# Attention with a relative bias and an ELU MLP: the second chunk pair made from seven products, and four smaller edits

## The chip, the cores and the metric

One Trainium2 chip, one of its cores. The metric is the time of one execution on the device in microseconds. The kernel before took 662.24 us (median of 3 runs, 661.66 to 663.11).

## The reference, cut to what matters

```python
# q, k, v: (4 batches, 8 heads, 576 positions, 64)
scores = matmul(q, k.T) / 8
x = log1p(|i - j|) / log1p(max(i, 1))                  # positions i, j
bias = relu(x * w1 + b1) @ w2                          # 32 hidden, one value per head
attn = softmax(scores + bias)
x = matmul(attn, v)                                    # -> 2304 tokens x 512
h = x @ w_in                                           # 512 -> 2048
g = where(h > 0, h, exp(min(h, 0)) - 1)
out = g @ w_out                                        # 2048 -> 512, float32
```

## The kernel before, in words

The work has three stages, one after another on the same engines. The order of instructions on each engine is the order in which the program writes them; the framework adds the waits and gives out buffers.

**Bias (`bias_phase`).** 36 sets of 16 rows each. For a set, four relu operations (L220 on ScalarE, L222 on VectorE, DVE for short; `LEAN` lists the sets of which ScalarE makes two instead of one), matmuls that mix the 32 hidden values into 8 heads (`mix`, L230), a scaled copy out of PSUM (`place`, L243, ScalarE) and a transfer into the bias tile (L251 for a set alone, L263 for two together). The last set goes head by head.

**Attention (`attention`).** 16 head pairs, one step each. A step is five strings of tokens (`FIRST` for the first pair, `STEPS` and `LATE` for the others, `LAST` behind the last pair); each token is a method. `S` makes scores on PE, `X` adds the bias and takes the extreme on DVE (L359) and the exponential on ScalarE (L370), `T` transposes on PE into two of three PSUM banks (the pool "w"), `P` copies those out on ScalarE (A) or DVE (V), `M` and `Q` do so for the middle columns, `V` multiplies by v, `C` copies the result. `a` means the pair of this step, `y` the one before. After each string `aside` adds more: for every fourth pair the sums of a batch are inverted and transposed (`lift`, `invert`, `turn`; L390 on PE, L392 on DVE) and stored. The tokens low, scale, sign, shift and add decode one float64 weight chunk per step (L313 and L326 on GpSimd, L317 to L323 on DVE); the result is stored to DRAM (L328, SP). Loads of decoded weights are `load_w` (L558); a weight is split into a high part on ScalarE (`high_w`, L561) and a low part on DVE (`low_w`, L565), because matmuls run in a reduced-precision format with three products per pair of operands.

**MLP (`mlp`).** Three token blocks of 768 (two halves of 384), each with 8 chunk pairs i, 24 pairs in all. The first `FIRST` pairs take `eight`: four blocks of x @ w_in, 12 matmuls each, from weights that attention has split. All others take `seven`: seven products of sums, 6 matmuls each, of sums of weight blocks (A11, A12, A22, S1 to S4, made by `make_w`: L824 to L829 the sums on DVE into the tile S, L821 the high parts on ScalarE, L822 the low parts on DVE) and sums of x (T1 to T4; L542, L551, L554). `make_w` is cut by `yield`, and `at(i, k, ...)` puts each piece behind product k of pair i. After a product come the ELU's steps: L899 and L900 on ScalarE, L893 (maximum) on DVE, the high copy to g L894 on ScalarE, the low part L888 on DVE, one or two products later. The matmuls with w_out (`second`, L865) of pair i - 1 fill in between the products of pair i; pair 0 has none to fill in. `seven` uses two PSUM tiles, "h0" and "h1", one buffer each: its first, third and the maximum of its third product free the tile of its fifth. Made weights are stored to DRAM (L846, L847) and fetched again in the second and third block (L803). The weight rings, "S" and "wa" of the pool wq lie where tiles of attention lay.

Of the kernel before, what the change touches and what calls it, by code (L numbers as in the profile page):

```python
# [11 lines left out]
F32R = mybir.dt.float32r  # L12
# [12 lines left out]
def kernel(  # L25
# [11 lines left out]
    nc = tc.nc  # L37
    B, HP, D, _, S = qT.shape
    NT, DM = out.shape
    H = 2 * HP  # L40
    P = 128
    NCH = S // P
# [8 lines left out]
    WW = 2 * DM  # L51
# [6 lines left out]
    keep = ctx.enter_context(tc.tile_pool(name="keep", bufs=2))  # L58
# [86 lines left out]
    def bias_phase():  # L145
        with (
# [8 lines left out]
            NS = S // 16  # L155
# [49 lines left out]
            sets = [(2 * o + y, s) for s in range(4) for y in range(2) for o in range(2)]  # L205
            sets += [(2 * o + y, s) for o in (2, 3) for s in range(4) for y in range(2)]
            sets[16:16] = [(2 * NCH, s) for s in range(4)]
            LEAN = 1, NS - 6, NS - 5, NS - 4
            rels, pss = {}, {}

            def relu(s):
                B, x = sets[s]
                rels[s] = []
                for g in range(4):
# [3 lines left out]
                    rel = (bw0, bw1, bw2)[s % 3].tile([P, S], F32, tag="rel", name="rel")  # L218
                    if g < (2 if s in LEAN else 1):
                        nc.scalar.activation(rel, src, AF.Relu, bias=b)  # L220
# [17 lines left out]
            def place(s):  # L238
                if s % 2 == 0:
                    pss["bo"] = bop.tile([P, 2, S], F32, tag="bo", name="bo")  # L240
                bo = pss["bo"]
                B, x = sets[s]
                nc.scalar.activation(  # L243
                    bo[:, s % 2].rearrange("p (f x) -> p f x", f=2), pss.pop(s)[:, :, 0:HS],
                    AF.Copy, scale=inv[:, B, x:x + 1],
                )
                if NCH <= B < 2 * NCH:
                    q0 = 64 * (B % 2) + x
                    dst = bias[q0:q0 + 61:4, B // 4, :, B // 2 % 2]
                    if s < NS - 1:  # L250
                        nc.sync.dma_start(out=dst, in_=bo[:, s % 2])  # L251
                        return
                    src = bo[:, s % 2].rearrange("(k h) x -> k h x", h=H)
                    parts = [(dst[:, h], src[:, h]) for h in range(H)]
                    later.extend(parts[2:])
                    send(parts[:2])
                    return
                if s % 2 == 0:
                    return
                B, x = sets[s - 1]  # L260
                if B < NCH:
                    q0 = 64 * (B % 2) + x
                    nc.sync.dma_start(out=bias[q0:q0 + 61:4, 0], in_=bo)  # L263
                    return
                for e in range(2):
                    src = bo.rearrange("(i e) s x -> i e s x", e=2)[:, e]
                    for o in range(2):
                        q0 = TAIL * e + x + o
                        nc.sync.dma_start(out=biast[q0:q0 + 61:4], in_=src[:, o])
# [109 lines left out]
    def invert(b):  # L379
        sm = st["sm", b].rearrange("p h u -> p (h u)")  # L380
        nc.vector.reciprocal(sm, sm)
# [174 lines left out]
    def load_w(fc, pool=None):  # L556
        wa = wab[fc] = (pool or keep).tile([P, WW], F32, tag="wa", name="wa", bufs=2)
        nc.sync.dma_start(out=wa, in_=wf[fc])  # L558

    def high_w(fc):  # L560
        nc.scalar.copy(ws[fc][0], wab[fc])  # L561

    def low_w(fc, eng):
        hi, lo = ws[fc]
        eng.tensor_sub(lo, wab.pop(fc), hi.bitcast(F32))  # L565


    room = bias.rearrange("p c h t x -> p (c h t x)").bitcast(F32R)
    RW = NCH * H * S
# [3 lines left out]
    for fc in range(4):  # L573
        o = RW // 2 + 2 * fc * WW
# [3 lines left out]
    def attention():  # L578
# [14 lines left out]
        )  # L593
        FIRST = (
            "aS0 aS4 aX00 aX01 high rest aX40",
            "aS1 aX10 aX11",
            "aS2 aT0 w3 aP00A aX20 aX21 aP01V",
            "aS3 aT1 w3 aX30 aX31 aP10V",
            "zS0 aT4 aP11V aP40A aP41A",
        )  # L600
        SECOND = (
# [9 lines left out]
        )  # L611
        LAST = (
            "yM0 yQ0V yT2 yP20A yP21V yV00 yV01 low",
            "yT3 yP30A yP31V yV02 yV03 sign yM1 yQ1A yV04 yC0V shift",
            "yV10 yV11 yV12 yV13 yV14 yC1A",
        )
        late = []

        V, G = nc.vector, nc.gpsimd
# [98 lines left out]
        def aside(n, i):  # L718
            if i == 1:
                weights(n - 2, "store")  # L720
            if i == 0 and n > 0:
                load_v(n)
                pad_v(n - 1)
            if i == 2:
                if 0 < n < NP - 2:
                    load_pair(n + 2)
            if n == 0 and i == 1:
                open_banks()
            if n > 0 and n % HP == 0:
                if i == 0:  # L730
                    lift(n // HP - 1)
                if i == 1:
                    invert(n // HP - 1)
                if i == 2:
                    late.extend(turn(n // HP - 1))
            others(n, i)
            if n < NP - 1:
                return
            if i == 0:
                load_w(0)  # L740
                load_w(1)
            if i == 2:
                high_w(0)
            if i == 3:
                low_w(0, nc.vector)
            if i == 4:
                load_w(2)
                high_w(1)
# [9 lines left out]
        pad_v(NP - 1)  # L758
        step(NP, LAST[0])
        invert(B - 1)  # L760
        step(NP, LAST[1])
        late += turn(B - 1)
        step(NP, LAST[2])
        others(NP, 1)
        low_w(1, nc.vector)
        flush()
        load_w(3)
        weights(NP - 1, "store")
        high_w(2)
        low_w(2, nc.vector)  # L770

    def mlp():
        ep = ctx.enter_context(tc.tile_pool(name="ep", bufs=3))
# [3 lines left out]
        wq = ctx.enter_context(tc.tile_pool(name="wq", bufs=1))  # L777
# [4 lines left out]
        AN, GN = 2 * 7 * AW, 4 * DM  # L782

        wrings = [
            [wq.tile([P, AN], F32R, name="wA0")] + [room[:, o:o + AN] for o in (RW // 2, RW // 2 + 4 * WW)],
            [wq.tile([P, GN], F32R, name=f"wB{i}") for i in range(3)],
        ]
        wA = [dpool.tile([P, AN], F32, name=f"wA{q}") for q in range(NQ)]
        wB = [dpool.tile([P, GN], F32, name=f"wB{q}") for q in range(NQ)]
        NP2 = NB * NQ  # L790
        FIRST = 2


        def place_w(i, kind):
# [54 lines left out]
        acc, count, g = {}, {}, {}  # L849


        def second(i, order):
            j = i // NQ
            for e, h in order:
                gh, gl = g[i, e]
                wh, wl = (
                    [ws[2 * i + e][f][:, DM:] for f in range(2)] if i < FIRST else [W2[i][:, f, e] for f in range(2)]
                )
                for t in range(3 * h, 3 * h + 3):
                    if (j, t) not in acc:  # L860
                        acc[j, t] = accp.tile([P, DM], F32, tag="acc", name="acc")
                        count[j, t] = 0
                    for x, w in ((gh, wh), (gh, wl), (gl, wh)):
                        count[j, t] += 1
                        nc.tensor.matmul(  # L865
                            acc[j, t],
                            lhsT=x[:, t * P:(t + 1) * P],
                            rhs=w,
                            start=(count[j, t] == 1),
                            stop=(count[j, t] == 6 * NQ),  # L870
                        )
                        if count[j, t] == 6 * NQ:
                            os = ep.tile([P, DM], F32, tag="os", name="os", bufs=4)
                            (nc.scalar.copy if t % 2 else nc.vector.tensor_copy)(os, acc[j, t])
                            t0 = 2 * j * HB + t * P
                            (nc.scalar if t % 2 else nc.sync).dma_start(out=out[t0:t0 + P, :], in_=os)
                        yield


# [98 lines left out]
        def at(i, k, fn, *args):  # L978
            plans.setdefault((i, k), []).append((fn, args))

        V, G = nc.vector, nc.gpsimd
# [2 lines left out]
        free = [slots[8], slots[1]]  # L984
        at(0, 0, sums_x, 0, ("T2",), V)
        at(0, 1, sums_x, 0, ("T4",), V)
        at(0, 1, high_w, 3)
        at(0, 2, low_w, 3, V)
        for (m, k), name in (((0, 2), "T2"), ((0, 3), "T3"), ((1, 1), "T1"), ((1, 2), "T4")):
            at(m, k, high_x, 0, name, xo[name], nc.scalar.copy)  # L990
            at(m + (k + 1) // 4, (k + 1) % 4, low_x, 0, name, xo[name], V)

        for i in range(FIRST, NQ + FIRST):
            q = i % NQ
            run = make_w(i)
            for e in range(2):
                at(i - 2, 0 if i - 2 < FIRST else 2, load_w, 2 * q + e, wq if i % 2 == 0 else keep)
            for k in (0, 0, 1, 2, 3, 3, 3) if i == FIRST else (0, 1, 2, 3, 4, 5, 6):
                at(i - 1, k, next, run)
            at(i, 0, next, run)  # L1000
            at(i, 1, next, run)
            at(i, 3, next, run, None)
# [14 lines left out]
        for j in range(1, NB):  # L1017
            o = (j - 1) * NQ
# [16 lines left out]
        for i in range(NP2):  # L1035
            j, q = divmod(i, NQ)
# [84 lines left out]
```

## Time and profile before

| what | value |
|---|---|
| median of 3 runs | 662.24 us |
| the profiled execution | 660.94 us, span 659.2 us |
| PE busy | 643.9 us (98%) |
| DVE busy | 479.5 us (73%) |
| ScalarE (ACT) busy | 449.6 us (68%) |
| GpSimd (POOL) busy | 142.7 us (22%) |
| granted TensorE clock | 0.999 |

The rows further down come from one profiled execution; times are microseconds from the start of its span. A row of a timeline gives start, duration, engine, line, operation, tiles and shapes, and in brackets how long the engine stood idle before and what ended that. A row of the chain gives start, length and the work that the end of the kernel was waiting for at that time. SPq and ACTq are the queues that issue transfers.

### The profile page before, as it was taken

Reading aid. Unit: us, or ns where it says so; the run is one execution under the profiler, and the core shown is the slowest. Engines: PE = TensorE matmul, PEld = TensorE weight load, DVE = VectorE, ACT = ScalarE, POOL = GpSimd, SP = SyncE. Lnnn points to the kernel's source line nnn. Section 1 sums busy time; section 2 is a strip of 40 time slices with the busy share of each in tenths; the row PEclk is TensorE's granted clock in tenths of the full one; section 3 lists DMA queues with packets and bytes.
Section 4 is the critical chain, followed back from the end, with each engine's and each line's share of the span. In section 5 each row is a group of like instructions: output and inputs, shape, how many; then the busy total and the mean of one; then the engine's idle time right before and its main releaser. Section 6 shows DMA issues by size and latency. Waiting matters only on the chain.

```text
span 659.2 us, 14000 instructions
## 1 busy us (share of the span) xinstructions
PE 643.9 (98%) x5316; PEld 517.3 (78%) x5316; DVE 479.5 (73%) x993; ACT 449.6 (68%) x981; POOL 142.7 (22%) x207
## 2 busy tenths in 40 slices
PE   6988999999999999999999999999999999999997
PEld 3335777777777677799998889899899899899896
DVE  7998888898888988986778998554466554444443
ACT  6999999999999899685666676544345544444443
POOL 1002666656665667500000000000000000000000
PEclk9999999999999999999999999999999999999999
DMA  6999677776888676546798678977854565444102
GB/s 166 215 223 253 178 206 235 245 235 206 227 269 235 190 200 219 204 174 213 252 360 291 240 254 337 373 265 239 279 211 191 198 254 231 184 178 176 65 0 96
DMA packets 47139, 144.42 MB, mean 219 GB/s; under 512 B 9936, under 2 KB 22624, under 8 KB 39392
## 3 DMA queue, kind: packets, MB, share of 16 engines
q1 hardware_dynamic: 45584, 140.88, 65.6%
q10 hardware_dynamic: 1488, 2.65, 1.1%
q8 instruction: 42, 0.69, 0.4%
q14 instruction: 25, 0.20, 0.1%
HBM read 91.92 MB, written 40.97 MB: 202 GB/s over the span
## 4 chain that ended last, share of the span: by engine, by line
PE 89%; ACT 6%; DMA 2%; issue 1%; SPq 1%; DVE 0%; ACTq 0%
PE acc L865 30%; PE h L914 27%; PE wv L468 13%; PE ps L339 11%; PE wt L427 6%; ACT rel L220 3%; ACT bo L243 3%; PE wm L401 1%; PE acc L914 1%; PE wt L435 1%; DMA bias<-bo 1%; DMA T<-in_rtab_dram 0%; DMA kk<-in_k_dram 0%; DMA out_dram<-os 0%; PE spin L707 0%
## 5 line engine op out<-in xcount | busy, mean ns | idle before, releaser
L865 PE MATMUL acc<-wB,gh 128*128 128x512 f32 x528 | 171.3, 392 | 0.0
L914 PE MATMUL h<-bias 128*128 128x384 f32 x552 | 111.4, 338 | 0.0
L865 PEld LDWEIGHTS acc<-wB,gh 128*128 128x128 f32 x528 | 98.1, 188 | 14.3
L359 DVE CUSTOM_DVE_ANT_0 ss<-ps,bias 128x576 f32<-128x576 f32 x128 | 91.8, 754 | 22.3 <-PE ps L339 10.9
L914 PEld LDWEIGHTS h<-bias 128*128 128x128 f32 x552 | 99.8, 188 | 7.5 <-issue 0.4
L865 PE MATMUL acc<-wB,gl 128*128 128x512 f32 x264 | 103.8, 393 | 0.0
L370 ACT ACTIVATE ss<-ss,nm 128x576 f32<-128x576 f32 x128 | 99.3, 778 | 5.1 <-DVE nm L359 4.8
L894 ACT CAST gh<-e 128x384 fp32r<-128x384 f32 x96 | 49.4, 514 | 39.8 <-DVE e L893 38.8
L899 ACT ACTIVATE e<-c 128x384 f32<-128x384 f32 x66 | 34.7, 525 | 53.4 <-DVE c L945 53.4
L888 DVE TENSOR_TENSOR gl<-e,gh 128x384 fp32r<-128x384 f32 x96 | 53.2, 554 | 19.0 <-ACT gh L894 16.6
L899 ACT ACTIVATE e<-h 128x384 f32<-128x384 f32 x28 | 13.8, 491 | 69.4 <-PE h L914 68.5
L893 DVE SCALAR_TENSOR_TENSOR e<-e,c 128x384 f32<-128x384 f32 x66 | 36.8, 557 | 30.6 <-ACT e L900 30.5
L914 PE MATMUL h<-bias,wA 128*128 128x384 f32 x276 | 56.3, 338 | 0.0
L865 PEld LDWEIGHTS acc<-wB,gl 128*128 128x128 f32 x264 | 49.5, 187 | 7.8
L914 PEld LDWEIGHTS h<-bias,wA 128*128 128x128 f32 x276 | 50.2, 188 | 3.8
L900 ACT ACTIVATE e<-e 128x384 f32<-128x384 f32 x96 | 50.5, 526 | 3.0
L945 DVE TENSOR_TENSOR c<-h,u 128x384 f32<-128x384 f32 x66 | 36.7, 556 | 20.1 <-PE h L914 20.1
L230 PE MATMUL bps<-rel,cs 128*32 128x288 f32 x576 | 43.9, 424 | 6.4 <-ACT rel L220 1.7
L427 PEld LDWEIGHTS wt<-ident,ss 64*128 64x128 f32 x1024 | 41.0, 138 | 10.9 <-issue 7.0
L427 PE MATMUL wt<-ident,ss 64*128 64x64 f32 x1024 | 46.7, 227 | 1.1 <-DVE nm L359 0.4
L373 POOL TENSOR_SCALAR md<-ss 128x128 f32<-128x128 f32 x64 | 21.9, 342 | 116.6 <-ACT ss L370 112.7
L339 PE MATMUL ps<-kh,qh 64*128 64x288 f32 x256 | 45.5, 341 | 0.1
(139 smaller groups left out, 1203.0 us busy)
## 6 DMA issues: line engine op xcount, KB each, us to landing
wB<-wB SPq DMA_DIRECT2D x22, 1024.0 KB, 5.2
raw<-in_wd_dram SPq DMA_DIRECT2D x16, 1024.0 KB, 6.4
bias<-wA SPq DMA_DIRECT2D x9, 1792.0 KB, 9.2
wA<-wA SPq DMA_DIRECT2D x8, 1792.0 KB, 8.7
wa<-wf SPq DMA_DIRECT2D x20, 512.0 KB, 4.4
wA<-bias SPq DMA_DIRECT2D x5, 1792.0 KB, 9.0
wf<-da SPq DMA_DIRECT2D x16, 512.0 KB, 7.0
qq<-in_q_dram SPq DMA_DIRECT2D x32, 144.0 KB, 6.2
```

The source lines that it names most:

```text
L230: nc.tensor.matmul(ps[32 * g:32 * g + 32, f, 0:HS], lhsT=W2, rhs=rel[g][:, f * HS:(f + 1) * HS], start=True, stop=True,)
L339: nc.tensor.matmul(ps[:, f, 0:HS], lhsT=(qh, ql)[q][r, u * P:(u + 1) * P] if u < NCH else qd[n % 2][q], rhs=k[r, f * HS:(f + 1) * HS], sta ...
L359: nc.vector.tensor_tensor_reduce(out=s.rearrange("p (f x) -> p f x", f=2), in0=st["ps", n, u][e][:, :, 0:HS], in1=bap.rearrange("p (f x) - ...
L370: nc.scalar.activation(s, s, AF.Exp, bias=nm, scale=-1.0, accum_out=st["sm", b][:, hp, col:col + 1])
L427: nc.tensor.transpose(banks[r][:, x * TAIL:(x + 1) * TAIL], ss[q, c:c + P], ident[q, q])
L468: nc.tensor.matmul(st["pv", n, half][e * D:(e + 1) * D, 0:N], lhsT=l, rhs=r, start=start, stop=stop)
L865: nc.tensor.matmul(acc[j, t], lhsT=x[:, t * P:(t + 1) * P], rhs=w, start=(count[j, t] == 1), stop=(count[j, t] == 6 * NQ),)
L888: nc.vector.tensor_sub(gl, t, gh.bitcast(F32))
L894: nc.scalar.copy(g[i, e][0][:, h * HB:(h + 1) * HB], t)
L899: nc.scalar.activation(t, src, AF.Relu, scale=-1.0)
L900: nc.scalar.activation(t, t, AF.Exp, scale=-1.0)
L914: nc.tensor.matmul(ps, lhsT=a[f][c], rhs=x[y][c], start=(start and k == 0), stop=(stop and k == len(todo) - 1), skip_group_check=not start,)
```

## The change

Five edits. `mlp`'s `FIRST` goes from 2 to 1: pair 1 takes `seven`, its weights are made behind the products of pair 0, chunks 2 and 3 are no longer split plainly, two of the weight rings' places change their order, and T1 to T4 are split one product earlier. `turn` comes one string later. The strings behind the last pair are reordered, with `low_w(1)` and `load_w(3)` ahead of the second. In the bias phase set 32 leaves `LEAN`, and the first two sets are sent one by one. The last output tile is copied and stored in two halves.

```diff
-            LEAN = 1, NS - 6, NS - 5, NS - 4
+            LEAN = 1, NS - 6, NS - 5
...
-                if NCH <= B < 2 * NCH:
+                if s < 2 or NCH <= B < 2 * NCH:
...
-            "aS3 aT1 w3 aX30 aX31 aP10V",
+            "aS3 aT1 w3 aP10A aX30 aX31",
...
         LAST = (
-            "yM0 yQ0V yT2 yP20A yP21V yV00 yV01 low",
-            "yT3 yP30A yP31V yV02 yV03 sign yM1 yQ1A yV04 yC0V shift",
-            "yV10 yV11 yV12 yV13 yV14 yC1A",
+            "yT2 yP20A yP21V yV00 yV01 low",
+            "yT3 yM0 yP31V yQ0A yP30A yV02 yV03 sign yV04 yC0V shift",
+            "yM1 yQ1A yV10 yV11 yV12 yV13 yV14 yC1A",
         )
...
-                if i == 2:
+                if i == 3:
                     late.extend(turn(n // HP - 1))
...
         step(NP, LAST[0])
         invert(B - 1)
+        low_w(1, nc.vector)
+        load_w(3)
         step(NP, LAST[1])
         late += turn(B - 1)
         step(NP, LAST[2])
         others(NP, 1)
-        low_w(1, nc.vector)
         flush()
-        load_w(3)
         weights(NP - 1, "store")
-        high_w(2)
-        low_w(2, nc.vector)
...
-            [wq.tile([P, AN], F32R, name="wA0")] + [room[:, o:o + AN] for o in (RW // 2, RW // 2 + 4 * WW)],
+            [wq.tile([P, AN], F32R, name="wA0")] + [room[:, o:o + AN] for o in (RW // 2 + 4 * WW, RW // 2)],
...
-        FIRST = 2
+        FIRST = 1
...
-                            (nc.scalar.copy if t % 2 else nc.vector.tensor_copy)(os, acc[j, t])
                             t0 = 2 * j * HB + t * P
-                            (nc.scalar if t % 2 else nc.sync).dma_start(out=out[t0:t0 + P, :], in_=os)
+                            ends = [(t % 2, slice(0, DM))]
+                            if t0 + P == NT:
+                                ends = [(k, slice(k * DM // 2, (k + 1) * DM // 2)) for k in range(2)]
+                            for k, c in ends:
+                                (nc.scalar.copy if k else nc.vector.tensor_copy)(os[:, c], acc[j, t][:, c])
+                                (nc.scalar if k else nc.sync).dma_start(out=out[t0:t0 + P, c], in_=os[:, c])
...
-        at(0, 1, high_w, 3)
-        at(0, 2, low_w, 3, V)
-        for (m, k), name in (((0, 2), "T2"), ((0, 3), "T3"), ((1, 1), "T1"), ((1, 2), "T4")):
+        for (m, k), name in (((0, 1), "T2"), ((0, 2), "T3"), ((0, 3), "T1"), ((1, 0), "T4")):
...
             for e in range(2):
-                at(i - 2, 0 if i - 2 < FIRST else 2, load_w, 2 * q + e, wq if i % 2 == 0 else keep)
+                if i > FIRST:
+                    at(i - 2, 0 if i - 2 < FIRST else 2, load_w, 2 * q + e, wq if i % 2 == 0 else keep)
```

## Rows read from the trace of the kernel before

**Rows 1.** The page's chain by line; busy time of each engine in two stretches.
```profile
PE acc L865 30%; PE h L914 27%; PE wv L468 13%; PE ps L339 11%; PE wt L427 6%; ACT rel L220 3%; ACT bo L243 3%; PE wm L401 1%; PE acc L914 1%; PE wt L435 1%; DMA bias<-bo 1%; DMA T<-in_rtab_dram 0%; DMA kk<-in_k_dram 0%; DMA out_dram<-os 0%; PE spin L707 0%
...
275.00:300.00 25.00, 25.00 (x133) 23.47 (x133) 21.13 (x31) 18.29 (x35) 3.56 (x1) 1.00 0.47 164
300.00:652.00 352.00, 352.00 (x1741) 316.52 (x1740) 216.73 (x392) 177.39 (x344) 0.00 (x0) 1.00 0.61 224
```

**Rows 2.** The chain in order of time at the MLP's start.
```profile
275.00 4.36 PE h L914 x24
...
283.52 2.08 PE h L914 x12
...
300.25 1.06 PE h L914 x6
301.31 1.15 PE acc L865 x5
```

**Rows 3.** Timeline of DVE, 274 to 292 us.
```profile
274.22 0.94 DVE L554 TENSOR_TENSOR bias<-xr,bias 128x768 fp32r<-128x768 f32 x1
275.08 1.21 DVE L565 TENSOR_TENSOR bias<-wa,bias 128x1024 fp32r<-128x1024 f32 x1
276.45 3.19 DVE L565 TENSOR_TENSOR bias<-wa,bias 128x1024 fp32r<-128x1024 f32 x1 [0.16 <-ACT bias L561]
...
284.58 0.55 DVE L888 TENSOR_TENSOR gl<-e,gh 128x384 fp32r<-128x384 f32 x1
285.05 0.55 DVE L893 SCALAR_TENSOR_TENSOR e<-e,acc 128x384 f32<-128x384 f32 x1
...
288.72 0.42 DVE L824 TENSOR_TENSOR S<-wa 128x256 f32<-128x256 f32 x1
...
291.12 0.69 DVE L822 TENSOR_TENSOR wA<-wa,wA 128x512 fp32r<-128x512 f32 x1
```

**Rows 4.** Timeline of GpSimd, the last decode.
```profile
270.84 1.18 POOL L313 TENSOR_SCALAR da<-raw 128x1024 f32<-128x1024 f32 x1
274.18 4.38 POOL L326 TENSOR_TENSOR da<-da,dm 128x1024 int32<-128x1024 int32 x1 [2.16 <-DVE da L323]
```

**Rows 5.** Timeline of SP's queue, the last decoded weight's store and the loads behind.
```profile
278.58 0.32 SPq L328 DMA_DIRECT2D wf<-da  x1
281.36 3.65 SPq L558 DMA_DIRECT2D wa<-wf  x4
```

**Rows 6.** Timeline of ScalarE, high_w(1) and the copies after it.
```profile
269.51 1.05 ACT L561 CAST bias<-wa 128x1024 fp32r<-128x1024 f32 x1
270.45 1.08 ACT L446 COPY ptb<-wt 128x512 f32<-128x512 f32 x2
```

**Rows 7.** The chain behind the last transpose T3.
```profile
270.19 1.23 PE wv L468 x8
```

**Rows 8.** The chain: batch turns and the steps around them.
```profile
106.75 1.77 PE wv L468 x12
...
113.18 0.22 PE wr L390
...
120.45 1.77 PE wv L468 x12
...
214.32 1.77 PE wv L468 x12
...
222.11 0.21 DVE rs L392
...
228.55 1.77 PE wv L468 x12
...
241.97 1.77 PE wv L468 x12
```

**Rows 9.** Engines and DMA at the bias phase's end; DVE's fourth block.
```profile
50.00:55.00 5.00, 4.13 (x61) 1.31 (x56) 4.05 (x11) 5.00 (x9) 0.00 (x0) 1.00 1.05 229
...
62.49 0.76 DVE L359 CUSTOM_DVE_ANT_0 ss<-ps,bias 128x576 f32<-128x576 f32 x1 [0.94 <-PE ps L339]
```

**Rows 10.** Timeline of ScalarE's queue, the last store.
```profile
655.97 0.34 ACTq L876 DMA_DIRECT2D out_dram<-os  x1
```

## Prediction

> **What bounds the kernel now.** First the chain that ended last: PE lines carry 89% of the span [rows 1]. Read in order of time it is PE without a hole from 59.7 us to the last store, so work taken from the other engines is worth nothing unless PE waits for it, and work given to them costs nothing until PE does. Second, the chain around the seam between attention and MLP [rows 2]: pair 0 of the MLP takes 8.52 us (275.00 to 283.52, its eight-product form has no second-layer work to interleave), pair 1 16.73 us (to 300.25), and each later pair seven times 1.06 + 1.15 us plus one more matmul, 15.7 us. Third, because PE is tight there only as long as its inputs come, the queues of the engines that feed it in that stretch: VectorE (DVE) [rows 3], GpSimd [rows 4], SP [rows 5] and ScalarE [rows 6]. DVE is the one to watch: it works 21.1 of the 25 us from 275 to 300, against 217 of the 352 us after that [rows 1]. The reader is to see that PE never waits at the seam today although DVE is nearly full there, because pair 1 is still made of plain products that need little of DVE.
>
> **Seven products for pair 1: what PE saves.** An eight-product pair issues 48 first-layer matmuls, a seven-product pair 42; six go, at 1.06 / 6 = 0.177 us each: -1.0 us (16.73 to 15.7) [rows 2].
>
> **What DVE must now do before PE can run pair 1.** Prices are start to start, which is 0.08 us under the duration: 0.86 us for 768 columns, 0.47 for 384, 0.34 for 256, 0.60 for 512, 1.14 for 1024 [rows 3]. low_w(2) and low_w(3) go (2.3 us), low_w(1) moves ahead. New in pair 0: four weight sums, the low parts of A11/A12, of the four sums and of A22, and T2's and T3's low parts one product earlier; T1's and T4's low parts, the two second-layer low parts and the sums for pair 2 land in pair 1's first products. Before, pair 1's 16.7 us stood between these two halves.
>
> I follow DVE's queue from the last row that is the same, high_w(1) on ScalarE, 269.51 to 270.56 [rows 6]. low_w(1), now ahead of the last copies, runs 270.58 to 271.72. The copy of the last scores' half (0.61) ends at 272.33. "scale" on GpSimd (270.84, 1.18 us [rows 4]) meets low_w(1) and ends at about 272.9; "sign" then takes 1.14 to 274.04; C0's copy 0.40, "shift" 0.60, the batch copy 0.20: 275.25. B22's low part 275.25 to 276.12, T2's difference to 277.0.
>
> GpSimd's "add" needs "shift" and comes next. In the trace it starts at 274.18, yet lasts 4.38 us [rows 4], because DVE's two subtractions (274.22, 275.08) run to 276.29 unhindered, and then low_w(2) takes 3.19 us instead of 1.21 [rows 3]: the two exclude each other, and DVE instructions that follow without a gap keep GpSimd out. So "add" runs from 277.0 for 276.29 to 278.56 = 2.2 us, to 279.2; its result is stored by SP at once, and the loads behind that store wait 2.78 us for its landing (278.58 to 281.36 [rows 5]): 282.0.
>
> **The wait that the change adds.** Those loads wait because their buffers lie where the decoded weight lay. Counted from the start of the attention's pools, the last decode's "da" has bytes 105,280 to 109,376; the MLP's wq pool gives bytes 102,400 to 106,496 to the first tile taken after its four rings. Before, that tile is "wa"; now make_w(1) takes its sums tile S first, inside pair 0. So DVE's second sum (the first, if the wait is for the whole tile) must wait for the store's landing at 282.0. DVE stands 5 us, and behind it stand pair 0's first ELU maximum, T4's difference and everything below; ScalarE's copies to g wait for those maxima. load_w(3), moved ahead on SP past three stores, is not the late one: issued at 272, landed by 277. Nothing behind it on SP is due before C0's store at 274.5.
>
> **From there to PE.** Pair 1's fifth product reuses the PSUM tile of its first; that tile is free when DVE has taken the ELU maximum of the third product. Ahead of that maximum stand, from 282.0: five subtractions of 768 columns (4.35), one of 1024 (1.14), four of 512 (2.4), nine of 256 (3.06, and 0.2 between dependent ones), nine of 384 (4.23): 15.4 us. ScalarE adds 1.8 us of waits, the largest (1.2) before A22's low part, whose high copy stands in one queue with pair 0's four ELUs and eight copies. So the maximum starts at 299.2 and PE's fifth product at 299.8. Three products with their second-layer matmuls follow, 6.9 us: the next pair starts at 306.7 instead of 300.1, +6.6 us with the saved matmuls counted. The same addition made for the kernel before gives every DVE start of rows 3 within 0.05 us.
>
> Without the wait for the store the same queue starts at 277.0 and passes the fifth product at 296.75: +3.55. That is the floor of this step, DVE's overload alone.
>
> A rule of the Trainium skill would place GpSimd's add earlier. Rows 3 and 4 show an add that started 0.04 us before DVE's subtraction and still lost. "SBUF — State Buffer", section "Who interferes with whom", says that whoever issues first holds the shared pair for the whole instruction and the other blocks. By that rule the add would run at 275.2 to 277.5 and the landing come 1.7 us sooner; by the rows it does not.
>
> **Order behind the last pair.** PE's order there loses nothing, but the mid transpose "yM0" now stands third in a pool of three banks: the last T3 took one of T2's, and the other is freed by P20A, which ScalarE runs at 270.45 behind high_w(1) [rows 6]. T3 would end at 269.8 (one transpose of 0.37 us earlier than 270.19 [rows 7]), yM0 starts at 271.05: 1.2 us of PE idle, pair 0 at 276.25. In the sum above it costs nothing more, since DVE decides; where DVE does not, it is +1.2 (0 to 1.9).
>
> **Batch turn.** The transpose itself costs 0.22 us. The three steps with it last 13.70, again 13.70 and 14.23 us against 13.42 for the next one [rows 8]: 0.28, 0.28, 0.81. In the third PE waited until DVE's copy at 222.11, behind two casts; one step later that copy follows the scores' reductions and the next transpose needs it some 0.8 us after. Together 1.37 us, of which three times 0.22 stay: -0.7 (bounds -0.9 and -0.1: the transpose hides too, or only the short stalls go). The store to rd goes one flush later; its first reader is in the next step.
>
> **Bias phase.** One relu of 0.66 us goes from ScalarE to DVE (0.44), which lets DVE start the first scores about 0.4 us earlier. But the DMA engines are full (1.05) and head 0 of the last rows lands then: DVE takes it at 62.49 after 0.94 us of idle time [rows 9], and I put the end of that wait down to the landing as much as to PE's scores. Sending the first set alone starts its 288 KB 1.3 us earlier, into a time when the engines are idle, and the next transfers still come when ScalarE has made them. I take 0 (-0.5 to +0.1). The first copy moved to ScalarE: 0, PE next waits for ScalarE's T4 copies.
>
> **Tail and weights.** The last store leaves at 655.97 [rows 10] and lands 2.2 us later; two halves leave at 655.8 and 655.9 with half the bytes: -0.2 (-0.5 to 0). Pair 9 is fetched instead of made: 0, behind PE.
>
> **Sum**, against the profiled execution's 660.94 us: +6.6 - 0.7 - 0 - 0.2 = +5.7, 666.6 us. That execution is 1.3 us below the median of the runs, so on the median's scale 662.24 + 5.7 = 667.9 us, and the rivals' times are given on it too.
>
> **Rivals.**
> - A, the sums tile doesn't wait (it lies elsewhere, or the store lands early): DVE's overload alone, +3.55 - 0.9 = +2.65, 664.9. For it: only that the layout is counted from code, no row shows S there. Against: the loads of rows 5 waited for just these bytes.
> - B, the add gets in front of B22's low part at 275.2 (in rows 3 and 4 only 0.04 us lie between the two starts) and ends at 277.5: the landing at 280.3, +4.9 - 0.9 = +4.0, 666.2. Against: the order of starts is the same as before, and there DVE won. (It is what the Trainium skill's rule, cited above, would give.)
> - C, faster: DVE keeps up. Then pairs 0 and 1 cost -1.0 us, and -0.7 and -0.2 stand: -1.9, 660.3. It decides at pair 1's fifth product: the third maximum must be done by 292.3, 7 us before my count. For it: in the old pairs 0 and 1 DVE had 3.9 us of idle time and ScalarE 6.7 [rows 1]. Against: from 275.25 to that point there are 17.1 us, and the queue above holds 17.1 us of DVE work and GpSimd's 2.2 before any wait.
> - D, as C, but PE waits for P20A in front of yM0: -1.9 + 1.2 = -0.7, 661.5, no change that can be measured.
>
> **Chances.** Forecast 0.42, B 0.13, A 0.23, C 0.13, D 0.09. Slower (over 0.2%, 1.3 us, about what a measurement of this kernel can tell from no change) is forecast, B and A: 0.78; same 0.09; faster 0.13. The range holds forecast, A and B with the bounds of turn, bias and tail: from 662.8 (A less 0.5 for the bias, and a part of the ScalarE waits) to 669.2 (forecast with the turn at -0.1 and 0.7 us more of waits); C and D are left out.
>
> **What will show it.** Right: DVE idle for some 5 us before a 128x256 sum near 277 to 282, released by the store wf<-da; PE idle before pair 1's fifth product, released by DVE, 3 us; PE idle 1.2 us before the mid transpose; batch steps of 13.6 us; DVE's first bias reduction earlier but the fourth block's still near 62.5. Wrong: the chain of waits still all PE from 275 us on, or seven-product pairs starting by 300 us.

## The result and the profile after

| | median | ratio to before |
|---|---|---|
| before | 661.95 us (661.15 to 663.11, 4 runs) | |
| after | 669.21 us (668.81 to 670.00, 4 runs) | 1.0108 [1.0095, 1.0121] |

The change is slower by 7.3 us where +5.7 was forecast (669.2 us against 667.9). The profiled execution of after took 669.15 us, span 667.3 us, granted clock 1.0.

The page's chain by line of after (before: [rows 1]):

```profile
PE acc L863 28%; PE h L916 24%; PE wv L468 12%; PE ps L339 10%; PE wt L427 5%; ACT rel L220 3%; ACT bo L243 3%; DMA out_dram<-os 1%; DMA bias<-bo 1%; PE wm L401 1%; PE wt L435 1%; POOLq L1118 0%; DMA wf<-da 0%; ACT ss L370 0%; DMA T<-in_rtab_dram 0%
```

And busy time of its engines in two stretches (PE, PEld, DVE, ACT, POOL, granted clock, DMA share, GB/s):

```profile
275.00:300.00 25.00, 20.28 (x105) 16.95 (x102) 18.90 (x34) 14.36 (x28) 3.17 (x1) 1.00 0.37 112
300.00:652.00 352.00, 350.42 (x1734) 315.20 (x1734) 213.82 (x384) 177.12 (x343) 0.00 (x0) 1.00 0.63 231
```

The chain has three new names, the store wf<-da, GpSimd's queue ahead of it and ScalarE's exponential (L370), and the output store out_dram<-os stands at 1% where it had 0%. PE, full in both stretches before, now has 4.7 us of holes in the first and 1.6 us in the second. The first lot is the forecast's seam. The second was not forecast.

**The seam.** The chain in order of time of after (start, length, work; it answers to [rows 2]):

```profile
274.91 3.27 POOLq L1118
278.20 2.93 DMA wf<-da
281.54 0.43 DVE S L822
...
299.37 1.33 PE h L916 x6
...
306.54 1.04 PE h L916 x6
```

Timelines of DVE, GpSimd and ScalarE in that stretch (with SP's store in the chain above they answer to [rows 3 to 6]):

```profile
274.99 0.94 DVE L554 TENSOR_TENSOR bias<-xr,bias 128x768 fp32r<-128x768 f32 x1
277.79 1.21 DVE L542 TENSOR_TENSOR T<-xr,xr 128x768 f32<-128x768 f32 x1 [1.86 <-DMA rd<-rs]
281.54 0.43 DVE L822 TENSOR_TENSOR S<-wa 128x256 f32<-128x256 f32 x1 [2.54 <-DMA wf<-da]
...
291.55 0.42 DVE L820 TENSOR_TENSOR wA<-wa,wA 128x256 fp32r<-128x256 f32 x1 [1.17 <-ACT wA L819]
...
298.77 0.55 DVE L895 SCALAR_TENSOR_TENSOR e<-e,h 128x384 f32<-128x384 f32 x1
...
274.95 3.22 POOL L326 TENSOR_TENSOR da<-da,dm 128x1024 int32<-128x1024 int32 x1 [2.17 <-DVE da L323]
...
281.30 0.62 ACT L819 CAST wA<-wa 128x512 fp32r<-128x512 f32 x1 [1.85 <-DMA wf<-da]
```

The reader is to see the path of the forecast: GpSimd's add ends at 278.2, SP stores its result, DVE's first sum starts when that has landed, then DVE works to the third maximum with one break of note (1.17 us, for ScalarE), and PE's fifth product of pair 1 follows 0.6 us behind it. Pair 2 starts at 306.54 instead of 300.25 [rows 2]: +6.3 us.

**The end of the first block** lies 120 us behind the seam, in a stretch that the forecast passed over. Timelines of after's DVE, ScalarE and SP's queue there:

```profile
420.19 0.69 DVE L877 COPY os<-acc 128x512 f32<-128x512 f32 x1 [3.85 <-DMA out_dram<-os]
...
421.46 0.58 ACT L877 COPY os<-acc 128x512 f32<-128x512 f32 x1 [3.76 <-DMA out_dram<-os]
...
401.26 0.32 SPq L801 DMA_DIRECT2D wB<-wB  x1
401.67 0.38 SPq L801 DMA_DIRECT2D wA<-wA  x1
402.15 0.38 SPq L844 DMA_DIRECT2D wA<-bias  x1
405.99 0.32 SPq L845 DMA_DIRECT2D wB<-wB  x1
412.38 8.87 SPq L878 DMA_DIRECT2D out_dram<-os  x3
```

Its chain:

```profile
415.79 5.59 DMA out_dram<-os
...
422.45 0.49 ACT p L959
...
422.98 1.32 PE h L916 x6
```

What SP's queue waited for from 398 to 425 us (total, times, longest), and its issues in the 25 us from 400 (count, size of one, median us from issue to landing):

```profile
SPq L801 <- PE acc L863: 11.0, 1, 11.0
...
out_dram<-os SPq DMA_DIRECT2D x3, 256.0 KB, 7.3
```

SP's queue of before at the same place, and its issues in the 25 us from 394:

```profile
393.60 0.32 SPq L803 DMA_DIRECT2D bias<-wA  x1
394.02 0.38 SPq L846 DMA_DIRECT2D wA<-wA  x1
...
407.24 4.40 SPq L876 DMA_DIRECT2D out_dram<-os  x3
411.73 0.46 SPq L803 DMA_DIRECT2D wB<-wB  x1
```

```profile
out_dram<-os SPq DMA_DIRECT2D x3, 256.0 KB, 2.2
```

Before, the first pair that is fetched is pair 10: its first-layer weights left at 393.60, pair 8's made weights were stored from 394.02 on, and the next fetch of each kind came behind the output stores (the second 0.55 us after the last row shown). After, pair 9 is fetched and no longer made, so the fetch of its second-layer weights stands in SP's queue ahead of all of these. It held the queue for 11.0 us, until PE's run at 399.84 had ended, and then this fetch, pair 10's (both L801) and the stores of pair 8's weights (L844, L845) left close together, 5632 KB within the 11 us ahead of the output stores. From 397.2 to 401.2 us the DMA engines had been busy 0.15 of the time, where before they were busy throughout (1.00). The second fetch landed 10.9 us after its issue, as the output stores began, so what those met of this were mostly pair 8's stores. The output stores take 7.3 us to land instead of 2.2, the four output buffers stay occupied, the copies of the fifth and sixth tile stand 3.8 us, and behind ScalarE's copy stands the copy p1 that PE's next product needs. From the last second-layer run of pair 7 to that of pair 9 the chain takes 33.35 us (399.84 to 433.19) where two pairs take 31.50: +1.85 us.

### The profile page after: what moved, and what is told of

It is laid out like the page before. It is cut to its first block, busy times and chain, and to the rows that moved or that the text cites. A ratio compares the mean times of both kernels' runs of the same rounds, so it can differ in the third digit from the quotient of the medians.

```text
span 667.3 us, 13995 instructions
## 1 busy us (share of the span) xinstructions
PE 645.2 (97%) x5310; PEld 516.8 (77%) x5310; DVE 479.2 (72%) x996; ACT 448.4 (67%) x981; POOL 143.7 (22%) x207
## 4 chain that ended last, share of the span: by engine, by line
PE 82%; ACT 8%; DMA 3%; DVE 3%; issue 2%; SPq 1%; POOLq 0%; POOL 0%; ACTq 0%; DVEq 0%
PE acc L863 28%; PE h L916 24%; PE wv L468 12%; PE ps L339 10%; PE wt L427 5%; ACT rel L220 3%; ACT bo L243 3%; DMA out_dram<-os 1%; DMA bias<-bo 1%; PE wm L401 1%; PE wt L435 1%; POOLq L1118 0%; DMA wf<-da 0%; ACT ss L370 0%; DMA T<-in_rtab_dram 0%
## 5 line engine op out<-in xcount | busy, mean ns | idle before, releaser
L863 PE MATMUL acc<-wB,gh 128*128 128x512 f32 x552 | 179.0, 392 | 0.0
L863 PEld LDWEIGHTS acc<-wB,gh 128*128 128x128 f32 x552 | 102.6, 188 | 15.0
L916 PE MATMUL h<-bias 128*128 128x384 f32 x540 | 109.8, 338 | 1.6 <-ACT p L959 1.6
L863 PE MATMUL acc<-wB,gl 128*128 128x512 f32 x276 | 108.6, 393 | 0.0
L916 PEld LDWEIGHTS h<-bias 128*128 128x128 f32 x540 | 97.9, 188 | 9.4 <-ACT p L959 2.0
L370 ACT ACTIVATE ss<-ss,nm 128x576 f32<-128x576 f32 x128 | 99.3, 779 | 6.3 <-DVE nm L359 5.8
L895 DVE SCALAR_TENSOR_TENSOR e<-e,c 128x384 f32<-128x384 f32 x69 | 38.5, 558 | 31.9 <-ACT e L902 31.8
L863 PEld LDWEIGHTS acc<-wB,gl 128*128 128x128 f32 x276 | 51.7, 187 | 8.2
L916 PEld LDWEIGHTS h<-bias,wA 128*128 128x128 f32 x270 | 48.6, 188 | 10.3 <-DVE e L895 4.1
L947 DVE TENSOR_TENSOR c<-h,u 128x384 f32<-128x384 f32 x69 | 38.4, 556 | 20.4 <-PE h L916 20.4
L339 PE MATMUL ps<-kh,qh 64*128 64x288 f32 x256 | 47.1, 341 | 0.2
```

Of the source, the lines that this page charges most:

```text
L339: nc.tensor.matmul(ps[:, f, 0:HS], lhsT=(qh, ql)[q][r, u * P:(u + 1) * P] if u < NCH else qd[n % 2][q], rhs=k[r, f * HS:(f + 1) * HS], sta ...
L370: nc.scalar.activation(s, s, AF.Exp, bias=nm, scale=-1.0, accum_out=st["sm", b][:, hp, col:col + 1])
L863: nc.tensor.matmul(acc[j, t], lhsT=x[:, t * P:(t + 1) * P], rhs=w, start=(count[j, t] == 1), stop=(count[j, t] == 6 * NQ),)
L916: nc.tensor.matmul(ps, lhsT=a[f][c], rhs=x[y][c], start=(start and k == 0), stop=(stop and k == len(todo) - 1), skip_group_check=not start,)
```

## The experiments

The first three take away one suspected cost each, from the changed kernel.

**sums_elsewhere.** The first sums get a place in the output tiles' ring, which is idle then; for this the output tiles become four parts of one tile.

```diff
-            [wq.tile([P, AN], F32R, name="wA0")] + [room[:, o:o + AN] for o in (RW // 2 + 4 * WW, RW // 2)],
+            [room[:, RW // 2 + 4 * WW:RW // 2 + 4 * WW + AN], wq.tile([P, AN], F32R, name="wA0"), room[:, RW // 2:RW // 2 + AN]],
...
-            S1 = wq.tile([P, 4, AW], F32, tag="S", name="S")
+            if i == FIRST:
+                S1 = oring[:, 2 * DM:].rearrange("p (s m) -> p s m", s=4)
+            else:
+                S1 = wq.tile([P, 4, AW], F32, tag="S", name="S")
...
+        oring = ep.tile([P, 4 * DM], F32, name="oring", bufs=1)
...
-                            os = ep.tile([P, DM], F32, tag="os", name="os", bufs=4)
+                            os = oring[:, len(sent) % 4 * DM:(len(sent) % 4 + 1) * DM]
```

> Changed kernel, but the first make's sums lie in the output tiles' ring (idle then) and the first A weights in the bias tile, so that nothing in pair 0's first products is the first write into the pool wq. Theory (5 us of DVE stand still because the pool's first write waits for the store wf<-da, all else is queue): DVE's first sum runs behind T2's difference at about 278.7 instead of 281.54, the third maximum of pair 1 at 295.9 instead of 298.77, the next pair starts at 302.3 instead of 305.15: -2.9, 666.3 us against 669.2. Rival (DVE's overload or ScalarE's copies set the end of pair 1 anyhow and the wait only filled their slack): no change, 669.2.

665.72 us, 1.0049 [1.0033, 1.0064] to before, where after has 1.0108. DVE and PE of its trace:

```profile
279.12 0.42 DVE L825 TENSOR_TENSOR oring<-wa 128x256 f32<-128x256 f32 x1
...
296.34 0.55 DVE L900 SCALAR_TENSOR_TENSOR e<-e,h 128x384 f32<-128x384 f32 x1
...
296.94 1.33 PE L921 MATMUL h<-bias 128*128 128x384 f32 x6 [1.51 <-DVE e L900]
```

The sum starts 2.4 us sooner, and so do the maximum and the fifth product (2.6 us, counted from high_w(1), which comes 0.2 us later in this trace): the wait is not slack, every part of it reaches PE. The medians differ by 3.5 us, the two profiled executions by 2.6. PE still waits 1.51 us for DVE there.

**sums_later.** Four sums and a low part for pair 2 behind the third maximum.

```diff
-            for k in (0, 0, 1, 2, 3, 3, 3) if i == FIRST else (0, 1, 2, 3, 4, 5, 6):
+            for k in (0, 0, 1, 2, 3, 3, 3) if i == FIRST else (2, 3, 4, 4, 5, 6, 6) if i == FIRST + 1 else (0, 1, 2, 3, 4, 5, 6):
```

> Changed kernel, but the seven pieces of make_w for pair 2 come behind products 2, 3, 4, 4, 5, 6, 6 of pair 1 instead of 0 to 6, so four sums and one low part (2.07 us of DVE) come behind the third maximum instead of ahead of it. Theory (the place in DVE's queue decides when pair 1's fifth product starts): maximum at 296.7 instead of 298.77, next pair at 303.1 instead of 305.15: -2.1, 667.1 us. Rival (pair 2's first products then wait for their own weights as long): 669.2.

667.50 us, 1.0075 [1.0059, 1.0090]; PE of its trace, pair 0's first product and pair 1's third and fifth:

```profile
275.09 4.43 PE L916 MATMUL h<-bias 128*128 128x384 f32 x24
...
292.13 1.31 PE L916 MATMUL h<-bias,wA 128*128 128x384 f32 x6 [0.78 <-ACT p L959]
...
296.83 1.23 PE L916 MATMUL h<-bias,wA 128*128 128x384 f32 x6
```

The fifth product starts 21.7 us behind pair 0's first, in after 23.4 (275.95 to 299.37): -1.7, and pair 2 keeps it. It is a little less than counted because that product then has no wait left at all; the last one that holds PE is the third's, for ScalarE's copy p1.

**fetch_late.** The two fetches behind the output stores again.

```diff
-            at(i - 2, 1, fetch_w, i, 0)
-            at(i - 1, 0, fetch_w, i, 1)
+            if i == NQ + FIRST:
+                at(i - 2, 1, fetch_w, i, 0)
+                at(i, 0, fetch_w, i, 1)
+            elif i == NQ + FIRST + 1:
+                at(i - 1, 0, fetch_w, i, 0)
+                at(i - 1, 1, fetch_w, i, 1)
+            else:
+                at(i - 2, 1, fetch_w, i, 0)
+                at(i - 1, 0, fetch_w, i, 1)
```

> Changed kernel, but pair 9's second-layer weights and pair 10's first-layer weights (2.8 MB) are fetched behind the first block's output stores. Theory (these fetches, issued 11 us ahead of the output stores, fill the DMA engines, the stores land in 5 to 9 us, and the output tiles' copies wait for them): stores land in 2 to 3 us, PE's hole of 1.6 us at 420 to 425 goes: -1.8, 667.4 us. Rival (the stores of pair 8's made weights, another 2.8 MB at 402 to 406, are enough for it): the hole stays, 669.2.

666.69 us, 1.0066 [1.0050, 1.0082]. In its chain two pairs take 31.50 us again (399.26 to 430.76), without a hole:

```profile
399.26 1.39 PE acc L863 x6
...
430.76 1.39 PE acc L863 x6
```

So the fetches are the cause. Pair 8's stores still go ahead of the output stores, but with no fetch in front they leave at 399.00 and 405.38, and the larger has landed 6.3 us later; there they do no harm. This run takes away the 2.8 MB of the fetches and the hold of the queue together, and does not tell which of the two does it. It is the term that the forecast had put at nothing. (By the medians the run gains 2.5 us; some 0.6 of them lie ahead of the seam, where after's profiled execution has the late load told of below.)

**add_first.** B22's low part behind T2's difference (B22 is a block of x that pair 0 reads).

```diff
-            (16, 1): [(low_x, 0, "B22", xo["B22"], V)],
+            (16, 1): [],
...
         at(0, 0, sums_x, 0, ("T2",), V)
+        at(0, 0, low_x, 0, "B22", xo["B22"], V)
```

> Changed kernel, but B22's low part on DVE comes behind T2's difference, so that GpSimd's add meets no DVE work in its first 2.8 us. Theory (a DVE subtraction holds GpSimd off even when the add has started): the add takes about 2.2 us instead of 3.22, its store lands and DVE's first sum starts 1.0 us sooner, at 280.5; pair 0 waits for B22's low part, but that time is free: -1.0, 668.2 us. Rival (the add is slow by itself, or the landing is not what decides): add 3.2 us, 669.2.

668.00 us, 1.0093 [1.0078, 1.0108]. GpSimd and DVE of its trace:

```profile
274.69 2.37 POOL L326 TENSOR_TENSOR da<-da,dm 128x1024 int32<-128x1024 int32 x1 [2.16 <-DVE da L323]
...
280.15 0.43 DVE L822 TENSOR_TENSOR S<-wa 128x256 f32<-128x256 f32 x1 [1.40 <-DMA wf<-da]
```

With no DVE subtraction in its first 1.9 us the add takes 2.37 us, not 3.22, and the sum starts 5.46 us behind the add's start instead of 6.59; 0.85 us of that are the add's own.

Next the three small edits, on the kernel before.

**side_only**: turn, bias phase and last tile, MLP and order as before (the diff is those hunks).

> Kernel before with three of the edits alone: the batch turn one string later with the first pair's order, the bias phase's two, the halved last tile. MLP and the order behind the last pair as before. Terms of the prediction: turn -0.7, bias 0, tail -0.2, so -0.9: 661.1 us against 662.0. Theory from the trace of the changed kernel: bias -0.2, the turn's two short stalls -0.3 but +0.4 elsewhere in the attention's steps, the third not shortened, tail 0: -0.1, 661.9 us (-0.5 to +0.2).

**660.72 us, 0.9974 [0.9962, 0.9986]**: the lowest median of the study, and faster than both kernels. The forecast's -0.9 holds; the theory read from the one trace of after does not.

**turn_only** and **bias_only** (each its hunks alone):

> Kernel before with the batch turn one string later and the first pair's copy order alone. Term of the prediction: -0.7, 661.25 us against 661.95; the steps with a turn last 13.55, 13.55 and 13.68 us instead of 13.70, 13.70 and 14.23. Rival (the gain of the three small edits together, 1.2 us, was the bias phase's and the tail's): 661.95.

661.70 us, 0.9992 [0.9980, 1.0003].

> Kernel before with the bias phase's two edits alone. Term of the prediction: 0 (-0.5 to +0.1), the time of the kernel before in the same session. Rival (the three small edits together gave 1.2 us, the turn alone 0.7, so the bias phase gives the rest): -0.5 to -1.0.

661.88 us, 0.9991 [0.9981, 1.0001]. Neither can be told from nothing by its time alone, and how the 1.2 us divide between them stays open. For the turn the traces decide, below.

**last_order**: side_only with the new strings behind the last pair.

> Kernel with the three small edits (turn, bias phase, last tile; 660.7 us), and the new order of the strings behind the last pair; low_w(1) and the loads stay where they were. Theory (the mid transpose waits for a bank that P20A frees behind high_w(1)): PE idle 1.2 to 1.4 us near 270, pair 0 starts 1.0 us later: +1.0, 661.7 us. Rival (the wait came with low_w(1) ahead of the copies on DVE, not with the order): 660.7.

661.72 us, 0.9992 [0.9981, 1.0004]. PE of its trace; after has the same row at 271.07, with the same 1.36 us:

```profile
270.32 0.44 PE L401 MATMUL wm<-ident,md 128*128 128x128 f32 x2 [1.36 <-ACT ptb L446]
```

The order costs 1.0 us where DVE does not hide it.

Last, the change with its waits mended, step by step.

**both**: the three of the first group together.

> The three undone costs together: the first sums outside the pool wq (-2.4 us in its own trace), pair 2's sums behind the third maximum (-2.1 counted), the first block's fetches behind its output stores (-1.8). Theory (they stand one behind the other on one path and add up): 669.2 - 6.3 = 662.9 us, pair 1's last second-layer run starts near 300.6 against 305.15 in the changed kernel. Rival (they share a part of the same wait, the sums moved later fill the time that the store's wait had left free): 664.5 us or more.

663.03 us, 1.0008 [0.9999, 1.0016]: they add up.

**best**: make_w's pieces for pair 1 regrouped, so that its four sums stand ahead of T2's difference and its second-layer low parts behind products 3 and 4 of pair 1.

```diff
...
+        run = make_w(FIRST)
+        at(0, 0, next, run)
+        at(0, 0, next, run)
         at(0, 0, sums_x, 0, ("T2",), V)
+        at(0, 0, next, run)
+        at(0, 1, next, run)
...
+        for k in ((0, 1), (0, 2), (0, 3), (1, 3), (1, 4)):
+            at(*k, next, run)
+        at(1, 5, next, run, None)
```

> As the combination of the three, and two more moves in DVE's queue: the four sums of pair 1 stand ahead of T2's difference (in the 1.9 us in which DVE waits for rd<-rs), and pair 1's two second-layer low parts (1.2 us) go behind products 3 and 4 of pair 1. Theory (all of the loss was DVE's queue, and what is left of it is at most 1.7 us): PE runs pairs 0 and 1 without a wait, pair 1's last second-layer run starts at about 298.5, and the kernel is 0.8 us under the one with the three small edits alone (660.7): 659.9. Rival (something else than DVE's queue, as ScalarE's copies, ends pair 1 too): 661.5 or more.

662.45 us, 1.0001 [0.9992, 1.0011]: the rival holds. PE and DVE of its trace:

```profile
290.24 1.31 PE L948 MATMUL h<-bias 128*128 128x384 f32 x6 [1.09 <-ACT p L991]
...
276.23 2.42 DVE L826 TENSOR_TENSOR oring<-wa 128x256 f32<-128x256 f32 x1
```

PE now waits for ScalarE's copy of pair 1's first product, which stands behind splits that the change moved into pair 0; and pair 0 starts 1.0 us late for the order behind the last pair. DVE gained nothing by the sums either, since GpSimd's add held the first of them for 2 us.

**best2** and **best3**: the old order behind the last pair and the second-layer high parts behind that copy; then T1's and T4's splits one product later, too (the hunk that best3 adds):

```diff
-        for (m, k), name in (((0, 1), "T2"), ((0, 2), "T3"), ((0, 3), "T1"), ((1, 0), "T4")):
+        for (m, k), name in (((0, 1), "T2"), ((0, 2), "T3"), ((1, 0), "T1"), ((1, 1), "T4")):
```

> As the last combination (662.45 us), with the two waits mended that its trace shows: the order behind the last pair as before the change (PE's mid transpose stood 1.36 us behind P20A, pair 0 started at 276.12 instead of 275.14), and the two second-layer high parts on ScalarE behind the copy of pair 1's first product instead of ahead of it (that copy held PE's third product 1.09 us). Theory (those two were what was left): pair 1's last second-layer run starts at 298.4 instead of 300.43, 660.4 us, at most 0.3 us from the kernel with the three small edits alone (660.7). Rival (other waits come up in their place): 662 or more.

661.17 us, 0.9983 [0.9973, 0.9993], between the two; the copy still held PE 0.92 us.

> As the version of 661.17 us, but T1's and T4's high and low parts one product later, as they stood before the change: T1's high copy (0.82 us) then stands on ScalarE behind the copy of pair 1's first product, which held PE's third product 0.92 us there. Theory (ScalarE's queue, full in pair 0, is what is left): PE's wait shrinks to 0.1 to 0.2 us, 660.4 us. Rival (T1's and T4's parts then come late for products 5 and 6): 661.2 or more.

660.93 us, 0.9979 [0.9969, 0.9989]. Its PE, pair 0's first product, the third of pair 1, and the first of pair 2:

```profile
274.03 4.45 PE L950 MATMUL h<-bias 128*128 128x384 f32 x24
...
287.31 1.31 PE L950 MATMUL h<-bias 128*128 128x384 f32 x6 [0.18 <-ACT p L993]
...
299.11 1.21 PE L950 MATMUL h<-bias,wA 128*128 128x384 f32 x6
```

PE of before in the same view, pair 0's first product and pair 2's:

```profile
274.93 4.43 PE L914 MATMUL h<-bias 128*128 128x384 f32 x24
...
300.08 1.23 PE L914 MATMUL h<-bias,wA 128*128 128x384 f32 x6
```

Pairs 0 and 1 take 25.08 us; before the change they took 25.15 (25.25 by the chain [rows 2]). So even here seven products for pair 1 give less than 0.1 us of the 1.0 that six matmuls are worth, and the kernel is as fast as the one with the small edits alone (660.72). Not every wait is gone: behind the one of 0.18 us, PE's fifth product starts at 292.13, as soon as DVE's third maximum (291.52) is done, and pair 1 takes 16.63 us (282.48 to 299.11) where pair 2 takes 15.75. A version without these two was not run.

## Why the prediction was near, and where it was wrong

| step | forecast | measured |
|---|---|---|
| first sum on DVE | 282.0 | 281.54 |
| third maximum | 299.2 | 298.77 |
| fifth product of pair 1 | 299.8 | 299.37 |
| next pair, against before | +6.6 | +6.3 |
| mid transpose yM0 starts, PE idle before it | 271.05, 1.2 | 271.07, 1.36 |
| turn, bias, last tile together | -0.9 | -1.2 by the medians of side_only |
| pair 9 fetched instead of made | 0 | +1.85 |

**The seam** came as forecast in place and nearly in price: DVE stands for the store, and from its first sum to the third maximum its queue takes 17.2 us, as counted (15.4 and 1.8). That the queue starts at the forecast time is in part luck. T2's difference was to follow B22's low part at 276.12; it waited for the store rd<-rs until 277.79, a wait that the forecast did not have. In this gap GpSimd's add went on and ended at 278.17, not 279.2; against that, its store took 2.93 us to land instead of 2.78, and the sum started 0.4 us behind the landing. PE's idle time, expected as 3 us ahead of the fifth product, is 1.51 us there, and 1.46 us already ahead of pair 1's first.

The two halves were told apart on the chip. The wait is 2.4 us of it (sums_elsewhere). Without it pair 2 starts at 304.11 by the chain, +3.9 (+3.7 counted from high_w(1)), close to the +3.55 that was forecast as a floor, for DVE's overload alone. But some 2.1 us of this are waits: in that trace too T2's difference waits for rd<-rs (1.69 us idle) and then lasts 1.38 us instead of 0.95 beside the add, so that the first sum comes at 279.12 and not at 277.0. Nor do the forecast's own terms give the floor: 277.0 + 15.4 + 1.8 + 0.6 is 294.8, not 296.75, and with that pair 2 would start 1.6 us late. So the overload alone is about 1.6 us (an estimate, 3.7 less 2.1), and that the floor was met is luck. Rival A, that nothing waits, is refuted by after's own row at 281.54; rivals C and D, that DVE keeps up, by the same queue.

One detail of the wait was wrong: it was put down to the tile S, by its bytes. Yet ScalarE's copy into wA0 (281.30), whose bytes by the same count lie below those of the decoded weight, waits for the same store, and T2's difference in another new pool waited for the store rd<-rs until 277.79. So it seems to be the first write into a pool that waits, for all that lay under any of it; the layout is counted from the code, and no row shows it. It made no difference here; that a first write into wq which is not S waits as long on DVE was not tried.

**Rival B** asked who wins between GpSimd's add and DVE. In after the add started at 274.95, 0.04 us ahead of B22's low part, and that low part still took its undisturbed 0.94 us, while the add took 3.22 instead of the 2.37 of add_first. So the add did not get in front, as B has it, and one DVE subtraction kept it out, as the forecast reads [rows 3, 4]. That two would do so was wrong: the second came only at 277.79, took 1.21 us instead of 0.95, and ended behind the add. The store landed at 281.13 (278.20 + 2.93), about midway between the forecast's 282.0 and B's 280.3. In `best` DVE paused 0.1 us after that low part, and its next sum, 0.42 us long elsewhere, lasted 2.42, to the end of the add. By the Trainium skill ("SBUF — State Buffer", section "Who interferes with whom") the one who issues first holds the pair for its whole instruction, which the page writes of DVE's two-port modes; T2's difference and the row of `best` agree with that, the add's 0.04 us of lead in after does not. Whether that start in the profile is already the add's claim on the pair, no run shows.

**Order behind the last pair.** Idle time and place were right to 0.2 us, and so was that DVE covers it. Its price without cover, 1.2 us, is 1.0 (last_order).

**Batch turn.** After's chain, and below it fetch_late's, which has the same attention (before: [rows 8]):

```profile
106.58 1.77 PE wv L468 x12
...
120.14 1.77 PE wv L468 x12
...
214.21 1.77 PE wv L468 x12
...
228.47 1.76 PE wv L468 x11
```

```profile
214.23 1.77 PE wv L468 x12
...
227.91 1.77 PE wv L468 x12
```

The first turn step takes 13.56 us as forecast. The third takes 14.26 in after, as if nothing were gained, and 13.68 in fetch_late. The cause stands in after's DVE:

```profile
213.70 0.69 DVE L317 TENSOR_SCALAR dm<-raw 128x1024 int32<-128x1024 uint32 x1 [0.51 <-DMA raw<-in_wd_dram]
```

A raw weight landed late in that one execution and put DVE back by 0.5 us. Of twelve traces with this edit, ten lack that wait and have 13.68 to 13.71 us there; after and side_only have it, and 14.26 and 14.34. So the term is 0.14 + 0.15 + 0.55 = 0.84 us; against it stand 0.17 us by which the last step but one ahead of the second turn is longer in the traces that have the bias phase's edits too (13.54 for 13.37). That makes -0.7.

**Bias phase and tail.** Zero was within what bias_only can tell (-0.6 us, -1.3 to +0.1). The tail's -0.2 did not come:

```profile
662.88 1.10 DVE L877 COPY os<-acc 128x512 f32<-128x512 f32 x2 [0.90 <-DMA out_dram<-os]
...
664.01 0.37 ACT L877 COPY os<-acc 128x256 f32<-128x256 f32 x1 [1.45 <-DVE os L877]
```

The two halves were counted side by side, but ScalarE's half waits for DVE's; what the smaller store gains (2.9 us from issue to the end of the span instead of 3.2 [rows 10]) the second copy uses up.

**The step that failed** is "Pair 9 is fetched instead of made: 0, behind PE". PE was busy there in before, so the fetches seemed covered; the forecast did not follow SP's queue to the block's end, though `FIRST`, which the diff changes, also bounds the loop that places the fetches. The fetch of pair 9's second-layer weights came to stand ahead of pair 8's stores and the output stores and held the queue for 11.0 us, and the four output buffers turned late landings into 1.85 us of PE's time, 1.58 of them idle. With it the sum is +6.6 - 0.9 + 1.8 = +7.5 on the median, 669.5; measured 669.2. Without it (fetch_late) the kernel lies 1.2 us under the forecast. The measured time lies at the upper end of the stated range, whose margin was meant for other terms: that it lies inside is luck, since the median of before, the seam and the small edits each came out 0.3 us lower than the forecast had them.

## What to carry to other kernels

A saving on the busiest engine is worth nothing in a stretch where the engines that feed it are full: six matmuls went, and the work that replaced them came where DVE and ScalarE had no time to spare. A first write into a pool that takes over old memory may wait for what lay under it (here 2.4 us for a store), so let a transfer or an engine with time to spare make it. When work turns from made into fetched, follow the transfer through its queue to whatever is issued behind it, however far from the edited place, and ask how long it stands there for its own buffer; and read small terms from several executions, since one late load in the profiled one can hide a real gain.

## What the runs showed that was not expected

- The load of a raw weight (1024 KB) landed late in single executions, and DVE waited for it: in the third turn's step above, and at the start of attention in turn_only (0.55 us of DVE idle at 68.23), where a stretch that takes 10.3 us in the other traces took 11.7.
- Stores of 256 KB took 2.2 us to land (median of three) where the last large transfer ahead of them had been issued 7.5 us before the first, and 7.3 us where 5632 KB had been issued in the 11 us before. In before, one issued 1 us behind two fetches took 11.2 us.
- Copies by two engines out of one PSUM tile into halves of one output tile ran one after the other (the rows on the tail); which of the two shared tiles makes the second wait was not tried.
